# Masked attention and a rational feed-forward layer on one core: other score products, other transfers of queries and keys, and another order

## The chip, the cores and the metric

The kernel runs on one core of a Trainium2 chip. The metric is the device time of one execution in microseconds (us); lower is better. The core has five engines that work side by side: TensorE (PE; its weight loads are PEld), VectorE (DVE), ScalarE (ACT), GpSimd (POOL) and SyncE (SP), which here only issues transfers. DMA engines move the data.

## The reference

There are two stages. The first is attention with a threshold, the second a feed-forward layer whose activation is a quotient of polynomials:

```python
batch, n_heads, seq, head_dim = (8, 8, 576, 64)
scores = scale * np.matmul(q, k.transpose(0, 1, 3, 2))
thresh = np.max(scores, axis=-1, keepdims=True) - tau
scores = np.where(scores >= thresh, scores, -1000000000.0)
attn = np.exp(scores - np.max(scores, axis=-1, keepdims=True))
attn = attn / (np.sum(attn, axis=-1, keepdims=True) + 1e-09)
x = np.matmul(attn, v)            # then laid out as (8 * 576, 512)

n_tokens, d_model, d_ff = (4608, 512, 2048)
h = x @ w_in
P = a[0] + a[1] * h + a[2] * h**2 + a[3] * h**3
Q = 1.0 + np.abs(b[0]) * np.abs(h) + np.abs(b[1]) * h**2
out = (P / (Q + 1e-6)) @ w_out
```

All inputs and the output are 32-bit floats.

## The kernel before

**Units and visits.** Heads go in pairs: 8 batches of 4 pairs, 32 pairs in all (index `bp`). The 576 query rows of a pair are four blocks of 128 and a rest of 64. A *unit* is one block of one pair. A full unit (`t < NT`, `NT` = 4) has 128 rows for both heads; the unit of the rest (`t == NT`) has the 64 rows of both heads on 128 partitions. There are 128 full units and 32 of the rest. Each batch is gone through in two rounds: a *visit* loads the queries and keys of a pair and does two of its blocks, or the two others and the rest (seven visits a batch, as the last pair does all in one). There are 56 visits.

**A unit.** `f_qk` computes the scores into three banks of PSUM, `f_max` their maximum (VectorE, line 815), `f_thr` the threshold, `f_pre` (ScalarE, line 830) and `f_sum` (line 834) the masked exponentials and their sums, `f_rec` the reciprocal, `f_hi` and `f_lo` (lines 339 and 856) the probabilities as two 16-bit halves, `f_tp` (line 866) turns each half by a transposing transfer on SyncE into the tile `pT`, and `f_av` (line 925) multiplies by V. Units of the first batch (`plain`) turn the probabilities on TensorE instead (lines 879 and 884). The score products of a full unit are two 32-bit products of 64 contraction rows, one per head, with 512 keys each (line 805), and one of all 128 rows for the last 64 keys of both heads (line 809). For that one the key tile has blocks of zeros, so that each head's rows meet only its own keys.

**Feed-forward.** `moe_ops` takes 256 tokens and 512 hidden columns at a time: 16-bit products (line 1042), the rational function on ScalarE and VectorE (lines 1051 to 1092), and 32-bit products (line 1101). It runs between the attention units, and for the last tokens alone at the end.

**Loads.** Two tiles QQ hold queries and two tiles KK hold keys (`NQ` = 2). `load_ops` issues three transfers for the queries of a visit and three for its keys, and two more of 16 KB where the visit has a unit of the rest. They are issued by SyncE for the first eight pairs (`EARLY_BP`), the keys of pairs 0 and 1 by ScalarE (`FROM_ACT`), and all others by GpSimd, whose queue also has the loads of V and of the weights and most stores.

**Order.** A planner (`Plan.order`) writes out the order of all instructions on each engine before the kernel is built. Each operation has an engine or a choice of two (`FLEX`), an assumed duration, a key and the buffers that it takes and gives back. The planner starts what can start first, and among near equals what has the lower key. `TURN` has an offset of the key for each group of operations, `KIND` one for each kind; `EARLY` and `PRICE` weigh ScalarE against VectorE where an operation may go to either. A transfer on SyncE (`"DMA"`) or GpSimd (`"GD"`) is taken to have landed 2.3 or 2.7 us after its assumed duration, however many others are under way; before 120 us (`LOADS_END`) transfers on SyncE that give a buffer back count double and one more.

Of the kernel before, what the change touches and what calls it, by code (L numbers as in the profile page):

```python
# [16 lines left out]
AX = mybir.AxisListType  # L17

# [19 lines left out]
SINGLE = 21  # L38
# [12 lines left out]

FROM_ACT = 2
# [25 lines left out]
EARLY = {"ACT": 1.2900, "DVE": 3.3863}  # L78
EARLY_END = 714.5248
PRICE = {"ACT": 1.0645, "DVE": 2.1978}  # L80

TURN = [
# [21 lines left out]
KIND = [  # L104
# [8 lines left out]
LOADS_END = 120.0  # L113
# [22 lines left out]
class Plan:  # L136
# [20 lines left out]
    def op(self, eng, dur, key, fn, after=(), take=(), drop=()):  # L157
        engs = {eng: dur} if isinstance(eng, str) else eng
        o = Op(engs, key, fn, [x for x in after if x is not None], list(take), list(drop))
        o.turn, o.kind = self.turn, self.kinds.setdefault(fn.__code__, len(self.kinds))  # L160
        turn = TURN[o.turn] / 1000 if o.turn < len(TURN) else 0.0
        o.key += turn
        o.key += KIND[o.kind] / 1000 if o.kind < len(KIND) else 0.0
        o.rank = self.rank + turn
        self.ops.append(o)
        return o
# [20 lines left out]
    def order(self):  # L187
# [19 lines left out]
        left = len(self.ops)  # L207
        while left:
# [38 lines left out]
            if e == "DMA" and o.drop and t < LOADS_END:  # L247

                o.dur = 2.0 * o.dur + 1.0
            free[e] = end = t + o.dur  # L250
            busy[e] += o.dur
            seen = end + self.LAT[e]
            for h in o.take:
                if h.sets is None:
                    slots = self.pools[h.pool]
                    h.slot = min(slots)[1]
                    slots.remove(min(slots))
                else:
                    h.bank = self.spot(h, t)[1]
                    for i in h.bank:  # L260
                        self.banks[i] = None
                if h.pool in line:
                    line[h.pool].pop()
# [8 lines left out]
            for d in o.then:  # L272
                d.wait -= 1
                for x in d.engs:
                    d.ready[x] = max(d.ready[x], end + (self.OWN[e] if x == e else self.TO.get((e, x), self.LAT[e])))
                    if not d.wait:
                        can[x].append(d)
# [12 lines left out]
def masked_attention_rational_ffn(  # L290
# [86 lines left out]
    QW = S + REM  # L377
    QQs = [const.tile([P, QW], F32, name=f"QQ{i}") for i in range(NQ)]
    KKs = [const.tile([P, QW + REM], F32, name=f"KK{i}") for i in range(NQ)]
    for t in QQs:  # L380
        nc.gpsimd.memset(t[:, NT * P:], 0.0)
    for t in KKs:
        nc.gpsimd.memset(t[0:D, S:QW], 0.0)
        nc.gpsimd.memset(t[D:P, 0:REM], 0.0)
# [96 lines left out]
    def decode_ops(i, key, load, hold, dst=None):  # L481
# [6 lines left out]
        def ld():  # L488
            if not loaded:

                for x in KKs[0][:, REM:REM + 1], QQs[0][:, 0:1]:
                    nc.gpsimd.tensor_scalar(cf[:, 15:16], x, 1.0, 1.0, ALU.mult, ALU.mult)
            if len(loaded) >= AHEAD and plan.now - loaded[-AHEAD][1] < RECENT:


                nc.gpsimd.tensor_scalar(cf[0:1, 15:16], loaded[-AHEAD][0][0:1, 0, 1:2].bitcast(F32), 1.0, 1.0, ALU.mult, ALU.mult)
            box["rw"] = load()
            loaded.append((box["rw"], plan.now))
# [26 lines left out]
        l = op("GD", 2.5, key - 2.0, ld, (), [hold])  # L525
# [112 lines left out]
    def load_ops(bp, ts):  # L638
# [7 lines left out]
        queue, eng = (nc.sync, "DMA") if bp < EARLY_BP else (nc.gpsimd, "GD")  # L646

        def ldq():
# [3 lines left out]
            queue.dma_start(QQ[D:P, S:], qT[bb, pr, :, S:S + REM])  # L652

        def ldk():
            KK = KKs[kh.slot]
            kq_ = nc.scalar if bp < FROM_ACT else queue
            kq_.dma_start(KK[0:D, REM:S], kT[bb, pr, :, 0:NT * P])
            kq_.dma_start(KK[D:P, REM:QW], kT[bb, pr, :, S + REM:])
            kq_.dma_start(KK[0:D, 0:REM], kT[bb, pr, :, NT * P:S])
            if NT in ts:  # L660
                for i in range(2):
                    kq_.dma_start(KK[i * D:(i + 1) * D, QW:], kT[bb, pr, :, NT * P + i * REM:S + i * REM])

        q_done[bp] = [op(eng, 4.3 if first else 1.6, p0, ldq, (), [qh])]
        k_done[bp] = [op(eng, 0.1 if bp < FROM_ACT else 1.6, p0 + 0.1, ldk, (), [kh])]

# [13 lines left out]
    def load_v_ops(bp):  # L680
# [25 lines left out]
        l = v_loaded[bp] = op(eng, 1.6, max(q, V0 + V1 * pr), ld, (), [vhold])  # L706
# [56 lines left out]
    def unit_ops(bp, t):  # L763
# [3 lines left out]
        single = units.index((bp, t)) < SINGLE  # L767
# [18 lines left out]
        def f_qk():  # L786
# [5 lines left out]
            if not full:  # L792

                s = box["s"][0] = s[:, 0:S]
                for k0, c0, n in (REM, 0, NT * P), (QW, NT * P, REM):
                    nc.tensor.matmul(s[:, c0:c0 + n], QQ[:, NT * P:QW], KK[:, k0:k0 + n], **one)
# [4 lines left out]
            for hh in range(2):  # L801

                r = slice(hh * D, (hh + 1) * D)
                d = s[:, 0:NT * P] if hh == 0 else s[:, w - NT * P:]
                nc.tensor.matmul(d, QQ[r, t * P:(t + 1) * P], KK[r, REM:S], **one)  # L805

            dst, src = (bass.AP(x.tensor, x.offset, [list(x.ap[0]), [n, 2], [1, REM]])
                        for x, n in ((s[:, NT * P:S], w - 2 * NT * P - REM), (KK[:, 0:REM], S)))
            nc.tensor.matmul(dst, QQ[:, t * P:(t + 1) * P], src, **one)  # L809
# [138 lines left out]
        qk = op("PE", 1.47 if full else 1.12, p, f_qk, need, [sh[0]], [kh, qh] * nh)  # L948
# [25 lines left out]
        else:  # L974
# [4 lines left out]
            if not full:  # L979
# [3 lines left out]
                    [hi_hold])  # L983
            tp = op("DMA", TPD if full else 0.6 * TPD, p + 0.65, lambda: f_tp("lo"), los + [tp], (), [e_hold])
# [25 lines left out]
    def moe_ops(ck, f0, nb, p, begins, ends, soon):  # L1010
# [161 lines left out]
        if ends:  # L1172
# [4 lines left out]
            for tt in range(2):  # L1177
# [9 lines left out]
                if through:  # L1187
                    op("DMA" if late else "GD", 0.6 if kind == "m" else 1.1, p + 2.3, lambda tt=tt: f_st(tt), [o], (), [ho])
# [95 lines left out]
```

## Time and profile before

| | |
|---|---|
| Median of 3 runs | 1310.31 us (1304.87 to 1311.28) |
| The profiled execution: time, span | 1312.41 us, 1310.6 us |
| Granted clock of TensorE, mean | 0.986 |
| Busy: TensorE, VectorE, ScalarE, GpSimd | 1253.8, 1217.9, 1114.4, 243.4 us |
| Mean busy share of transfers: queue of SyncE and ScalarE, queue of GpSimd | 37.4%, 16.4% of 16 engines |
| Moved | 146.66 MB, of which 60.30 read from HBM and 9.44 written |

The profile is of one execution; a busy time is the time in which at least one instruction of the engine ran. Ends of matmuls are modelled. A row of a timeline begins with the start (us from the first instruction), then the time, the engine, the line and the operation, and "x4" means four merged instructions. An engine name with a q (SPq) is its queue, where it issues transfers. A 32-bit product of line 805 or 809 stands as two records, one for each of its two passes.

### The profile page before, as it was taken

The numbers are of one execution on the slowest core, as the hardware profiler recorded it, in microseconds if no ns is written. First come the engines' busy times: TensorE is split into PE (matmuls) and PEld (weight loads), VectorE is DVE, ScalarE is ACT, GpSimd is POOL, SyncE is SP. The second block draws the span as 40 slices with busy tenths as digits, with TensorE's granted clock in tenths as the row PEclk, the third lists the DMA queues.
The fourth block names the chain that finished last, engine by engine and source line by source line (L and its number), as shares of the span: only waits on it lengthen the run. The fifth ranks groups of instructions, "written<-read, shape, count | busy, mean of one in ns | idle before, by whom it ended". The sixth has DMA issues, their size and how long they took to land. (4 is left out here: it accounts for less than half of the span.)

```text
span 1310.6 us, 25351 instructions
## 1 busy us (share of the span) xinstructions
PE 1253.8 (96%) x9430; PEld 931.8 (71%) x9430; DVE 1217.9 (93%) x1913; ACT 1114.4 (85%) x2182; POOL 243.4 (19%) x462
## 2 busy tenths in 40 slices
PE   8898989999999999998999979999999999999998
PEld 6576677777677777776777657766677777778886
DVE  5899999999999999988999979999999999999777
ACT  5898998999999999997999878978998798885564
POOL 1101100023213220323112231223213221110000
PEclk8998999999999999999999989999999999999999
DMA  7433454476656565677554875676756654563000
GB/s 206 132 116 125 142 128 87 105 160 119 124 116 134 124 131 107 117 143 129 95 103 96 115 132 100 122 126 119 137 106 115 132 131 75 109 111 55 17 17 17
DMA packets 340587, 146.66 MB, mean 112 GB/s; under 512 B 316208, under 2 KB 323184, under 8 KB 340464
## 3 DMA queue, kind: packets, MB, share of 16 engines
q1 hardware_dynamic: 316400, 86.49, 37.4%
q0 software_dynamic: 22784, 57.31, 16.4%
q8 instruction: 74, 1.21, 0.4%
q10 hardware_dynamic: 1280, 1.25, 0.4%
q14 instruction: 49, 0.40, 0.1%
HBM read 60.30 MB, written 9.44 MB: 53 GB/s over the span
## 5 line engine op out<-in xcount | busy, mean ns | idle before, releaser
L1101 PE MATMUL banks<-wp,g 128*128 128x512 f32 x1728 | 442.1, 404 | 1.6 <-DVE g L1092 1.2
L1042 PEld LDWEIGHTS <-wi 128*128 128x128 f16 x3456 | 333.6, 98 | 67.1 <-issue 29.0
L1042 PE MATMUL banks<-x,wi 128*128 128x256 f16 x3072 | 360.8, 274 | 10.0 <-ACT t L1051 9.3
L1101 PEld LDWEIGHTS banks<-wp,g 128*128 128x128 f32 x1728 | 315.9, 189 | 75.3 <-DVE g L1092 4.0
L834 ACT ACTIVATE e<-e,cf 128x576 f32<-128x576 f32 x288 | 222.1, 778 | 0.2
L856 DVE SCALAR_TENSOR_TENSOR e<-e,st,hi 128x576 f16<-128x576 f32 x252 | 204.6, 812 | 7.5 <-ACT hi L339 6.4
L339 ACT ACTIVATE hi<-e,st 128x576 f16<-128x576 f32 x223 | 169.6, 769 | 46.8 <-DVE st L845 30.8
L830 ACT ACTIVATE e<-banks,st 128x576 f32<-128x576 f32 x288 | 206.3, 737 | 3.0 <-DMA pT<-e 0.8
L815 DVE TENSOR_REDUCE st<-banks 128x2 f32<-128x1152 f32 x128 | 172.4, 1347 | 16.2 <-PE banks L809 15.8
L805 PE MATMUL banks<-KK,QQ 64*128 64x512 f32 x512 | 154.0, 650 | 7.2 <-DVE t L346 3.9
L925 PE MATMUL banks<-pT,V 128*64 128x256 f16 (+1 forms) x2520 | 122.8, 250 | 12.8 <-DMA pT<-e 10.2
L1051 ACT ACTIVATE t<-banks,hsc 128x512 f32<-128x512 f32 (+1 forms) x192 | 106.1, 574 | 30.3 <-PE banks L1042 24.5
L925 PEld LDWEIGHTS <-V 128*64 128x64 f16 x2520 | 105.0, 111 | 34.0 <-issue 22.7
L809 PEld LDWEIGHTS banks<-KK,QQ 128*128 128x128 f32 x256 | 38.6, 190 | 99.1 <-issue 94.6
L1078 DVE SCALAR_TENSOR_TENSOR t<-t,co,t 128x1024 f32<-128x1024 f32 (+1 forms) x73 | 92.3, 1265 | 17.4 <-ACT t L1072 17.1
L1069 ACT ACTIVATE t<-t,co 128x1024 f32<-128x1024 f32 (+1 forms) x73 | 82.8, 1134 | 29.6 <-DVE t L1065 24.1
L1092 DVE TENSOR_TENSOR g<-t,g 128x512 fp32r<-128x512 f32 x144 | 95.0, 684 | 3.1 <-ACT g L331 2.9
L650 POOL DMA_DIRECT2D QQ<-in_qT_dram x42 | 22.2, 529 | 381.0 <-PE banks L809 194.8
L1084 DVE SCALAR_TENSOR_TENSOR t<-t,co,t 128x1024 f32<-128x1024 f32 (+1 forms) x73 | 92.3, 1265 | 0.6
L1075 DVE SCALAR_TENSOR_TENSOR t<-t,co,t 128x1024 f32<-128x1024 f32 (+1 forms) x73 | 92.2, 1264 | 0.1
L1065 DVE SCALAR_TENSOR_TENSOR t<-t,co 128x1024 f32<-128x1024 f32 (+1 forms) x73 | 92.3, 1264 | 0.0
L1062 DVE SCALAR_TENSOR_TENSOR t<-t,co 128x1024 f32<-128x1024 f32 (+1 forms) x73 | 92.2, 1263 | 0.0
(128 smaller groups left out, 1545.3 us busy)
## 6 DMA issues: line engine op xcount, KB each, us to landing
t<-in_w_in_dram POOLq DMA_DIRECT2D x16, 512.0 KB, 5.3
t<-in_w_out_dram POOLq DMA_DIRECT2D x16, 512.0 KB, 4.1
out_dram<-u POOLq DMA_DIRECT2D x26, 256.0 KB, 2.9
V<-in_v_dram POOLq DMA_DIRECT2D x24, 256.0 KB, 4.5
QQ<-in_qT_dram POOLq DMA_DIRECT2D x42, 144.0 KB, 2.8
KK<-in_kT_dram POOLq DMA_DIRECT2D x42, 144.0 KB, 3.2
QQ<-in_qT_dram POOLq DMA_DIRECT2D x42, 128.0 KB, 2.9
KK<-in_kT_dram POOLq DMA_DIRECT2D x42, 128.0 KB, 2.8
```

The lines of the kernel that those rows point to most:

```text
L339: nc.scalar.activation(dst, src, AF.Identity, scale=factor)
L805: nc.tensor.matmul(d, QQ[r, t * P:(t + 1) * P], KK[r, REM:S], **one)
L815: nc.vector.tensor_reduce(box["st"][:, 0:2], box["both"], AX.X, ALU.max, negate=True)
L830: nc.scalar.activation(ev(hh), box["s"][hh], AF.Prelu, scale=SCALE, bias=box["st"][:, 2 + hh:3 + hh], alpha=STEEP)
L834: nc.scalar.activation(e, e, AF.Exp, scale=passes, accum_out=box["st"][:, 4 + hh:5 + hh])
L856: nc.vector.scalar_tensor_tensor(box["lo"][:, c], ev(hh), box["st"][:, 6 + hh:7 + hh], box["hi"][:, c], ALU.mult, ALU.subtract)
L925: nc.tensor.matmul(dst, V[:, c * P + hh * D:c * P + (hh + 1) * D], rhs, start=c == 0 and n == 0, stop=c == NT and n == 2)
L1042: nc.tensor.matmul(d, wi_tile(c, f0 + j, hl), x[:, c, :], start=c == 0 and n == 0, stop=c == NC - 1 and n == 2)
L1051: nc.scalar.activation(box["h3"][:, 2 * k:2 * k + 2, sl], psv[:, :, sl], AF.Identity, scale=hsc[:, b2, g:g + 1])
L1065: nc.vector.scalar_tensor_tensor(box["q"], box["q"], bc, box["q"], ALU.add, ALU.mult)
L1092: nc.vector.tensor_tensor(fr(g[:, 1]), box["r"][:, k * GW:(k + 1) * GW], g[:, 0], ALU.subtract)
L1101: nc.tensor.matmul(acc[tt], fr(g[:, x]), fr(wo[f][y]), start=begins and j == n == 0, stop=ends and j == nb - 1 and n == 2)
```

## The change

Full units' scores become four products of 64 contraction rows: 64 keys of the first head, 512 of the second, 512 of the first, 64 of the second. The two products of 64 keys write one PSUM bank, so an empty instruction on TensorE before the fourth waits for the first. The key tile loses its blocks of zeros and its second copy of the last 64 keys. Each head's keys come in one transfer; the third transfer of the queries is issued only where the visit has a unit of the rest. All queries and keys are issued by SyncE (`EARLY_QK` = 32), but for the keys of the first visits of pairs 0 and 1, which stay with ScalarE; V, weights and stores stay where they were. In the planner, transfers carry a `wire` pair: the first number is time on a wire that all of them share, the second the time from then to landing. All numbers of `TURN`, `KIND`, `EARLY` and `PRICE` are new, except `EARLY_END`. The change's name also speaks of sums of exponentials in SBUF.

```diff
+EARLY_QK = 32
-EARLY = {"ACT": 1.2900, "DVE": 3.3863}
+EARLY = {"ACT": 1.4369, "DVE": 3.4200}
-PRICE = {"ACT": 1.0645, "DVE": 2.1978}
+PRICE = {"ACT": 1.0733, "DVE": 2.2524}
...
-LOADS_END = 120.0
+BEGIN = 1.4
...
-            if e == "DMA" and o.drop and t < LOADS_END:
-
-                o.dur = 2.0 * o.dur + 1.0
             free[e] = end = t + o.dur
             busy[e] += o.dur
             seen = end + self.LAT[e]
+            if o.wire is not None:
+                wire = max(wire, t + BEGIN) + o.wire[0]
+                seen = max(wire, end + 1.0) + o.wire[1]
...
-                    d.ready[x] = max(d.ready[x], end + (self.OWN[e] if x == e else self.TO.get((e, x), self.LAT[e])))
+                    d.ready[x] = max(d.ready[x], seen if o.wire is not None else
+                                     end + (self.OWN[e] if x == e else self.TO.get((e, x), self.LAT[e])))
...
-    QW = S + REM
-    QQs = [const.tile([P, QW], F32, name=f"QQ{i}") for i in range(NQ)]
-    KKs = [const.tile([P, QW + REM], F32, name=f"KK{i}") for i in range(NQ)]
+    QQs = [const.tile([P, S + REM], F32, name=f"QQ{i}") for i in range(NQ)]
     for t in QQs:
         nc.gpsimd.memset(t[:, NT * P:], 0.0)
-    for t in KKs:
-        nc.gpsimd.memset(t[0:D, S:QW], 0.0)
-        nc.gpsimd.memset(t[D:P, 0:REM], 0.0)
+    KKs = [const.tile([P, S], F32, name=f"KK{i}") for i in range(NQ)]
...
-        queue, eng = (nc.sync, "DMA") if bp < EARLY_BP else (nc.gpsimd, "GD")
+        act = bp < FROM_ACT and ts[0] == 0
+        queue, eng = (nc.sync, "DMA") if bp < EARLY_QK else (nc.gpsimd, "GD")
...
-            queue.dma_start(QQ[D:P, S:], qT[bb, pr, :, S:S + REM])
+            if NT in ts:
+                queue.dma_start(QQ[D:P, S:], qT[bb, pr, :, S:S + REM])
 
         def ldk():
-            KK = KKs[kh.slot]
-            kq_ = nc.scalar if bp < FROM_ACT else queue
-            kq_.dma_start(KK[0:D, REM:S], kT[bb, pr, :, 0:NT * P])
-            kq_.dma_start(KK[D:P, REM:QW], kT[bb, pr, :, S + REM:])
-            kq_.dma_start(KK[0:D, 0:REM], kT[bb, pr, :, NT * P:S])
-            if NT in ts:
-                for i in range(2):
-                    kq_.dma_start(KK[i * D:(i + 1) * D, QW:], kT[bb, pr, :, NT * P + i * REM:S + i * REM])
+            kq_ = nc.scalar if act else queue
+            for hh, c in (0, 0), (1, S + REM):
+                kq_.dma_start(KKs[kh.slot][hh * D:(hh + 1) * D, :], kT[bb, pr, :, c:c + S])
...
-            for hh in range(2):
-
+            for hh, k0, n, d0 in (0, NT * P, REM, NT * P), (1, 0, NT * P, w - NT * P), (0, 0, NT * P, 0), (1, NT * P, REM, w - S):
                 r = slice(hh * D, (hh + 1) * D)
-                d = s[:, 0:NT * P] if hh == 0 else s[:, w - NT * P:]
-                nc.tensor.matmul(d, QQ[r, t * P:(t + 1) * P], KK[r, REM:S], **one)
-
-            dst, src = (bass.AP(x.tensor, x.offset, [list(x.ap[0]), [n, 2], [1, REM]])
-                        for x, n in ((s[:, NT * P:S], w - 2 * NT * P - REM), (KK[:, 0:REM], S)))
-            nc.tensor.matmul(dst, QQ[:, t * P:(t + 1) * P], src, **one)
+                if d0 == w - S:
+
+                    tc.add_manual_dep(nc.tensor.nop().ins, shared.ins.name, ORDERED, reason="one bank")
+                mm = nc.tensor.matmul(s[:, d0:d0 + n], QQ[r, t * P:(t + 1) * P], KK[r, k0:k0 + n], **one)
+                if d0 == NT * P:
+                    shared = mm
...
-        qk = op("PE", 1.47 if full else 1.12, p, f_qk, need, [sh[0]], [kh, qh] * nh)
+        qk = op("PE", 1.36 if full else 1.12, p, f_qk, need, [sh[0]], [kh, qh] * nh)
```

The tables `TURN` and `KIND` are left out here. The `wire` pairs are (0.75, 1.0) for queries, keys and stores, (0.95, 1.5 or 2.5) for V, (1.75, 2.0) for a weight block and (1.2, 0.8) for a transpose of a full unit, (0.65, 0.8) for one of the rest.

More of the change, by code (lines that the diff above doesn't have):

```diff
@@ L17 @@
 AX = mybir.AxisListType
+ORDERED = mybir.DependencyInfo(mybir.DependencyClass.Sync, mybir.DependencyReason.DATA)
 REBIAS = 2.0 ** -112
@@ L155, in pool, with op @@
         self.pools[name] = [(0.0, i) for i in range(n)]
-    def op(self, eng, dur, key, fn, after=(), take=(), drop=()):
+    def op(self, eng, dur, key, fn, after=(), take=(), drop=(), wire=None):
         engs = {eng: dur} if isinstance(eng, str) else eng
         o = Op(engs, key, fn, [x for x in after if x is not None], list(take), list(drop))
+        o.wire = wire
         o.turn, o.kind = self.turn, self.kinds.setdefault(fn.__code__, len(self.kinds))
@@ L206, in order @@
         done, busy = [], dict.fromkeys(engines, 0.0)
-        left = len(self.ops)
+        left, wire = len(self.ops), 0.0
         while left:
@@ L489, in ld @@
             if not loaded:
-                for x in KKs[0][:, REM:REM + 1], QQs[0][:, 0:1]:
+                for x in KKs[0][:, 0:1], QQs[0][:, 0:1]:
                     nc.gpsimd.tensor_scalar(cf[:, 15:16], x, 1.0, 1.0, ALU.mult, ALU.mult)
@@ L523, in f6 @@
                 tensor_tensor(dst.bitcast(I32), t, box["rw"][:, :, 0], ALU.add)
-        l = op("GD", 2.5, key - 2.0, ld, (), [hold])
+        l = op("GD", 2.5, key - 2.0, ld, (), [hold], wire=(1.75, 2.0))
         if i < NC:
@@ L651, in ldq @@
             queue.dma_start(QQ[D:P, 0:NT * P], qT[bb, pr, :, S + REM:])
-            queue.dma_start(QQ[D:P, S:], qT[bb, pr, :, S:S + REM])
+            if NT in ts:
+                queue.dma_start(QQ[D:P, S:], qT[bb, pr, :, S:S + REM])
         def ldk():
-            KK = KKs[kh.slot]
-            kq_ = nc.scalar if bp < FROM_ACT else queue
-            kq_.dma_start(KK[0:D, REM:S], kT[bb, pr, :, 0:NT * P])
-            kq_.dma_start(KK[D:P, REM:QW], kT[bb, pr, :, S + REM:])
-            kq_.dma_start(KK[0:D, 0:REM], kT[bb, pr, :, NT * P:S])
-            if NT in ts:
-                for i in range(2):
-                    kq_.dma_start(KK[i * D:(i + 1) * D, QW:], kT[bb, pr, :, NT * P + i * REM:S + i * REM])
-        q_done[bp] = [op(eng, 4.3 if first else 1.6, p0, ldq, (), [qh])]
-        k_done[bp] = [op(eng, 0.1 if bp < FROM_ACT else 1.6, p0 + 0.1, ldk, (), [kh])]
+            kq_ = nc.scalar if act else queue
+            for hh, c in (0, 0), (1, S + REM):
+                kq_.dma_start(KKs[kh.slot][hh * D:(hh + 1) * D, :], kT[bb, pr, :, c:c + S])
+        issue = {"DMA": 1.25, "GD": 1.1}[eng]
+        q_done[bp] = [op(eng, 3.1 if first else issue + (0.6 if NT in ts else 0.0), p0, ldq, (), [qh], wire=(0.75, 1.0))]
+        k_done[bp] = [op(eng, 0.1 if act else issue, p0 + 0.1, ldk, (), [kh], wire=(0.75, 1.0))]
+    place_of = {u: i for i, u in enumerate(units)}
     def is_plain(bp, t):
@@ L705, in load_v_ops @@
         q = bp * (NT + 0.5) - 17.0
-        l = v_loaded[bp] = op(eng, 1.6, max(q, V0 + V1 * pr), ld, (), [vhold])
+        l = v_loaded[bp] = op(eng, 1.7, max(q, V0 + V1 * pr), ld, (), [vhold], wire=(0.95, 1.5 if eng == "DMA" else 2.5))
         hv = [Hold("u", 1)]
@@ L766, in unit_ops @@
         full = t < NT
-        single = units.index((bp, t)) < SINGLE
+        single = place_of[bp, t] < SINGLE
         heads = (0, 1) if full else (0,)
@@ L794, in f_qk @@
                 s = box["s"][0] = s[:, 0:S]
-                for k0, c0, n in (REM, 0, NT * P), (QW, NT * P, REM):
-                    nc.tensor.matmul(s[:, c0:c0 + n], QQ[:, NT * P:QW], KK[:, k0:k0 + n], **one)
+                for c0, n in (0, NT * P), (NT * P, REM):
+                    nc.tensor.matmul(s[:, c0:c0 + n], QQ[:, NT * P:], KK[:, c0:c0 + n], **one)
                 return
@@ L982, in unit_ops @@
             tp = op("DMA", TPD if full else 0.6 * TPD, p + 0.6, lambda: f_tp("hi"), his + two["tp"], [two["pT"]] if t % 2 == 0 else (),
-                    [hi_hold])
-            tp = op("DMA", TPD if full else 0.6 * TPD, p + 0.65, lambda: f_tp("lo"), los + [tp], (), [e_hold])
+                    [hi_hold], wire=(1.2 if full else 0.65, 0.8))
+            tp = op("DMA", TPD if full else 0.6 * TPD, p + 0.65, lambda: f_tp("lo"), los + [tp], (), [e_hold], wire=(1.2 if full else 0.65, 0.8))
             two["tp"].append(tp)
@@ L1187, in moe_ops @@
                 if through:
-                    op("DMA" if late else "GD", 0.6 if kind == "m" else 1.1, p + 2.3, lambda tt=tt: f_st(tt), [o], (), [ho])
+                    op("DMA" if late else "GD", 0.6 if kind == "m" else 1.1, p + 2.3, lambda tt=tt: f_st(tt), [o], (), [ho], wire=(0.75, 1.0))
                 else:
```

49 rows, old and new, of tables (KIND, TURN) are left out of this document.

## The prediction

> **What bounds the kernel now.** I read the page's head first, then busy time by stretch, then the waits of each engine, then the instructions around one score product and one late transpose.
>
> ```profile
> span 1310.6 us, 25351 instructions
> PE 1253.8 (96%) x9430; PEld 931.8 (71%) x9430; DVE 1217.9 (93%) x1913; ACT 1114.4 (85%) x2182; POOL 243.4 (19%) x462
> ```
>
> Columns of the next view, by stretch: length, then busy time (and count) of PE, PEld, DVE, ACT, POOL, then TensorE's granted clock, the DMA engines' share and GB/s.
>
> ```profile
> 0.00:100.00 100.00, 87.08 (x583) 63.72 (x584) 80.69 (x198) 81.05 (x180) 14.14 (x43) 0.95 0.51 150
> 100.00:700.00 600.00, 580.74 (x4427) 427.21 (x4426) 576.93 (x905) 547.54 (x1088) 118.44 (x217) 0.99 0.59 122
> 700.00:800.00 100.00, 90.03 (x700) 65.75 (x699) 87.83 (x134) 79.27 (x165) 27.66 (x50) 0.95 0.63 111
> 800.00:1170.00 370.00, 360.47 (x2779) 264.73 (x2779) 358.19 (x545) 323.40 (x617) 82.05 (x150) 1.00 0.61 117
> 1170.00:1310.00 140.00, 135.49 (x960) 110.39 (x954) 114.25 (x135) 83.17 (x137) 1.12 (x2) 1.00 0.14 29
> ```
>
> TensorE and VectorE are both nearly full from 100 to 1170 us (97% and 96% in the first long stretch), so a saving on one alone is worth about half until the other stops it. The end (from 1170 us) is feed-forward alone, with TensorE at 97%; nothing of the change acts there but the order. What could be won by order alone is what both lose: TensorE is idle for 57 us of the span, VectorE for 93. The waits say how much of it hangs on transfers (columns: who waited, for whom: us in total, times, longest):
>
> ```profile
> PE banks L925 <- DMA pT<-e: 10.2, 9, 5.2
> PE banks L1042 <- ACT t L1051: 9.8, 8, 2.6
> DVE x L941 <- ACT x L935: 9.9, 3, 6.1
> ACT u L703 <- DMA V<-in_v_dram: 10.1, 9, 3.8
> ACT hi L339 <- DMA pT<-hi: 9.1, 3, 3.5
> ACT pT L331 <- issue: 2.3, 1, 2.3
> POOL QQ L650 <- PE banks L809: 194.8, 20, 25.7
> ```
>
> Of line 866, the transposes, the view of one line says who waited for them and how long one takes to land:
>
> ```profile
>   PE banks L925: 11.6, 10
>   ACT hi L339: 9.1, 3
> DMA to landing us min/median/max: 2.5/3.4/11.3
> ```
>
> Ten of 280 transposes come too late for TensorE, 11.6 us in all, and ScalarE loses 9.1 us to three. The largest, 5.2 us, has its cause beside it:
>
> ```profile
> 748.67 0.53 POOL L657 DMA_DIRECT2D KK<-in_kT_dram  x1
> 754.42 0.53 POOL L650 DMA_DIRECT2D QQ<-in_qT_dram  x1 [4.18 <-PE banks L809]
> 753.26 2.37 SPq L866 DMA_TRANSPOSE pT<-e  x1
> ```
>
> Two visits' queries and keys go out within 10 us, and the transpose between them takes 2.37 us to issue instead of its usual 1.3. The old plan, for which a transfer lands 2.3 us after it ends on its queue whatever else is moving, can't see that.
>
> **The change part by part.** *The score products.* Durations: one group on TensorE, its inner starts, and what follows it.
>
> ```profile
> 602.84 0.70 PE L805 MATMUL banks<-KK,QQ 64*128 64x512 f32 x2
> 603.37 0.60 PE L805 MATMUL banks<-KK,QQ 64*128 64x512 f32 x2
> 603.90 0.38 PE L809 MATMUL banks<-KK,QQ 128*128 128x128 f32 x1
> 604.11 0.28 PE L809 MATMUL banks<-KK,QQ 128*128 128x128 f32 x1
> 604.14 0.48 PE L1101 MATMUL banks<-wp,g 128*128 128x512 f32 x1
> 861.82 1.13 PE L805 MATMUL banks<-KK,QQ 64*128 64x512 f32 x4
> 863.21 1.47 PE L1042 MATMUL banks<-x,wi 128*128 128x256 f16 x12
> 410.45 1.13 PE L805 MATMUL banks<-KK,QQ 64*128 64x512 f32 x4
> 411.92 0.63 PE L925 MATMUL banks<-pT,V 128*64 128x256 f16 x8
> ```
>
> A product is two passes. The two heads' 64-row products run side by side: both first passes start at 602.84, both second ones at 603.37. A first pass of 512 columns takes 0.53 us, one of 128 columns 0.21 (603.90 to 604.11), so a column costs 0.32/384 = 0.83 ns and the rest, the weight load, 0.107. A second pass has its load under the first: 0.107 + 2 x 0.427 = 0.96 for the 512 columns, then 0.10 until 603.90, the change from half rows to full rows, then another bare load and 2 x 0.107. From the group's start to the next group's it is 1.30 us (before line 1101), 1.39 (line 1042), 1.47 (line 925).
>
> New, per half: one product of 64 columns and one of 512. Load 0.107, passes of 0.053; the next loads (0.107) are only half hidden under these, 0.054 bare each; then 2 x 0.427: 0.107 + 0.053 + 0.054 + 0.053 + 0.054 + 0.854 = 1.175, and 0.10 for the change back to full rows, which now comes after the group instead of inside it: 1.27. Against 1.30, 1.39 and 1.47 that is 0.03, 0.12 or 0.20 saved, and as the next group's first weight load then lies bare, where it was partly hidden, less than that before lines 1042 and 1101. I take 0.06 of bounds 0 and 0.20: with 128 groups (256 records of line 809), 8 us of TensorE time, half of which reaches the end: **-4**. On the bad side, if nothing overlaps as above, a half takes 2 x 0.160 + 2 x 0.533 = 1.39, plus 0.10: 1.49, which is 0.02 to 0.19 lost.
>
> The wait (an empty instruction before the fourth product, until the first is done, as both write one bank) holds all of TensorE's queue behind it. The first is over after 0.27 us, the second and third run to 0.96 and 1.17, so 0.7 us of work covers it; without that cover it would cost what the signal takes, 128 times. I put it at 0. VectorE's maximum waits for the same end of the group as before.
>
> The Trainium skill speaks against this part: TensorE: Matmul & The Clock Gate, "Part 3: Packing small matmuls", says that matmuls start and end strictly in program order. By it the third product could not start before the second's second pass. In the rows above the second head's first pass starts with the first head's first, ahead of that one's second pass, which bears more on products than on passes; so it stays a rival below.
>
> *The loads.* Rows of the groups and of two queues:
>
> ```profile
> L650 POOL DMA_DIRECT2D QQ<-in_qT_dram x42 | 22.2, 529 | 381.0 <-PE banks L809 194.8 <-PE banks L796 181.8 <-PE banks L1101 4.4
> L662 POOL DMA_DIRECT2D KK<-in_kT_dram x48 | 26.0, 552 | 0.2 <-issue 0.2
> 72.44 0.60 SPq L651 DMA_DIRECT2D QQ<-in_qT_dram  x1
> L866 SPq DMA_TRANSPOSE pT<-hi x140: 1200/1292/2063, 177.3 to 1189.2; - x140
> 45.81 2.16 ACTq L662 DMA_DIRECT2D KK<-in_kT_dram  x2
> ```
>
> After the first eight head pairs there are 42 visits with six issues each and 48 more small ones: 300 issues on GpSimd. They become 42 x 4 + 24 = 192 on SyncE at 0.60 us, 115 us. SyncE has 280 transposes at 1.3 (364 us) and some early loads, so it is under half full; what counts is what stands behind what. A load of a visit holds SyncE for 4.6 x 0.60 = 2.7 us, and longer if its buffer isn't free yet; behind it stand transposes, and behind these TensorE's line 925. On GpSimd such a load stands for long (194.8 us on line 809 alone), with V's loads, the weights and the stores behind it: those go free, and ScalarE waits 10.1 us for V. The bytes stay as they were but for the second copy of the last 64 keys. ScalarE issues 12 transfers less; five of them (43.86 to 48 us) kept it from a ready copy for 2.3 us. For the first load, one 16 KB transfer less of queries and of keys saves about 0.6 us before the first product. I take **-2** for ScalarE, **-1** for V and the start. Move to SyncE by itself: between -5 (all of V's wait that lies before a busy ScalarE) and +23 (rival below); I take 0, as the planner now orders these loads between the transposes with its own times for them. Removed memsets on GpSimd lie at the start under the first loads: 0.
>
> The skill's DMA: Bandwidth & Descriptors, "Issuing engines are not separate DMA queues", says that transfers of all issuing engines share the same 16 DMA engines, and only issue time is saved. The trace agrees: 2.8 us to landing for queries from GpSimd, 3.2 from SyncE:
>
> ```profile
> QQ<-in_qT_dram POOLq DMA_DIRECT2D x42, 144.0 KB, 2.8
> QQ<-in_qT_dram SPq DMA_DIRECT2D x14, 144.0 KB, 3.2
> ```
>
> *The plan.* Its transfers now queue for one wire, and all offsets and prices are new. No row shows the new order; bounds are what the old one loses: 11.6 + 9.1 = 21 us to late transposes on the good side, and as much again on the bad side, since the new table fits a model too. Nearest is the wait of TensorE itself, which is on a full engine; I take most of it, **-9**. *Sums of exponentials in SBUF*: lines 834 and 839 already sum into the tile st, which lies in SBUF, and the diff leaves them; so 0.
>
> Sum: -4 - 2 - 1 - 9 = -16. The profiled execution took 1312.4 us (span 1310.6 and 1.8 around it), 0.2% above the median of 1310.3: **1296**.
>
> **The rivals.** (a) *The order wins more*: all 21 us of late transposes go, 0.10 us or more of each group (13), 2 of ScalarE: -36 at full worth, -30 with VectorE in the way: 1281. For: both engines idle together at 760 us. Against: VectorE at 96% has no work taken off it. (b) *No change*: VectorE binds, the score saving vanishes and late transposes only move: 1307, give or take 4. For: the 9.8 us behind line 1051 and most other waits have nothing to do with transfers. (c) *SyncE as the bound, slower*: loads stand ahead of transposes, 42 x 2.7 = 115 us of delay handed to pT; if a fifth of it reaches TensorE, +23, less 7 for the rest: 1328. It decides from the point where more than one visit in ten finds pT with less than 2.7 us to spare; today ten transposes of 280 have none. (d) *Products in program order, slower*: 1.49 us a group, 0.10 to 0.19 more for the usual followers, 128 x 0.14 = 18 us on TensorE, of which three quarters reach the end (13), less 5 for the order: 1320. This is also the time that the page's rule would give.
>
> **How the numbers follow.** Forecast 0.42 (its own range 1287 to 1303), (a) 0.18, (b) 0.20, (c) 0.12, (d) 0.08. Half a per cent, about what a measurement here tells from no change, is 1303.8 to 1316.9. Faster 0.42 + 0.18 = 0.60, same 0.20, slower 0.20. Leaving out half of (a) and the worse half of (c) and (d), the range is 1274 to 1322.
>
> **What would show it.** The score group: four products with all starts of the third about 0.3 us after the group's, and 1.27 us to the next group; 1.49 says (d). On SyncE: direct transfers between transposes; TensorE's wait for pT under 5 us says the plan term is right, over 20 says (c). GpSimd's wait on QQ gone, ScalarE's 2.3 us gone. TensorE's busy time near 1246 and VectorE's unchanged. The forecast is wrong if TensorE's and VectorE's idle times in 100 to 1170 us stay as they are, or if a new wait for KK or QQ appears before the scores.

## The result, and the profile after

The changed kernel took 1291.05 us (median of 4 runs, 1289.5 to 1296.84) against 1309.2 us for the kernel before on the same chip (median of 4 runs): a ratio of 0.9886, 95% interval 0.9855 to 0.9917. That is 18 us faster, and 5 us under the forecast of 1296. The profiled execution took 1291.3 us, with a span of 1289.5.

The head of the page, and busy time by stretch in the same stretches and columns as before:

```profile
span 1289.5 us, 25792 instructions
PE 1233.6 (96%) x9668; PEld 966.1 (75%) x9668; DVE 1218.6 (95%) x1935; ACT 1110.6 (86%) x2159; POOL 83.8 (6%) x159
```

```profile
0.00:100.00 100.00, 83.75 (x567) 66.28 (x568) 81.33 (x201) 82.20 (x182) 14.80 (x41) 0.91 0.52 153
100.00:700.00 600.00, 581.09 (x4633) 451.60 (x4633) 585.39 (x929) 549.17 (x1082) 38.15 (x66) 1.00 0.59 121
700.00:800.00 100.00, 94.25 (x796) 73.59 (x795) 94.21 (x152) 86.02 (x168) 9.58 (x16) 1.00 0.52 109
800.00:1170.00 370.00, 360.34 (x2918) 280.73 (x2916) 362.87 (x557) 331.50 (x631) 21.23 (x36) 0.99 0.61 119
1170.00:1289.00 119.00, 114.19 (x762) 93.86 (x760) 94.84 (x100) 61.68 (x100) 0.00 (x0) 1.00 0.08 21
```

VectorE does the same work in less time: 1218.6 us busy against 1217.9, so its idle time fell by 22 us, most of it between 100 and 800 us. TensorE lost 20 us of busy time and kept its idle time, 56 us against 57. Looked at from TensorE alone, the whole gain would be shorter products; this reading is one of the theories below, and it is wrong.

The waits and the transposes (the last three rows are from the view of line 865, the transposes):

```profile
PE banks L1041 <- ACT t L1050: 8.2, 9, 1.4
PE banks L1100 <- ACT u L1111: 7.1, 2, 5.5
PE banks L806 <- DMA KK<-in_kT_dram: 3.6, 3, 1.6
PE banks L806 <- DMA QQ<-in_qT_dram: 2.9, 2, 2.1
ACT u L703 <- DMA V<-in_v_dram: 0.8, 1, 0.8
SPq L651 <- PE banks L796: 87.6, 22, 28.1
SPq L651 <- PE banks L806: 63.7, 20, 19.5
  ACT hi L343: 4.7, 3
  PE banks L924: 2.1, 3
DMA to landing us min/median/max: 2.5/3.3/6.7
```

TensorE's wait for late transposes fell from 11.6 to 2.1 us, ScalarE's from 9.1 to 4.7, and the latest transpose lands after 6.7 us instead of 11.3. ScalarE's wait for V fell from 10.1 to 0.8. The loads now stand on SyncE for 151 us until their buffer is free, with transposes behind them, and nothing shows that this hurts. One sign that the prediction named against itself did appear: TensorE's products wait 6.5 us for keys and queries in front of the scores, against 0.8 before (its weight loads waited 5.3 us then and 1.8 now). 5.8 of the 6.5 us lie in the first 28 us. One group of score products (rows of a timeline that overlap one moment each, so "x3" are those then running):

```profile
697.30 0.70 PE L806 MATMUL banks<-KK,QQ 64*128 64x64 f32 x2
697.57 1.07 PE L806 MATMUL banks<-KK,QQ 64*128 64x512 f32 x3
697.84 0.81 PE L806 MATMUL banks<-KK,QQ 64*128 64x512 f32 x4
698.58 0.50 PE L1100 MATMUL banks<-wp,g 128*128 128x512 f32 x1
```

The group starts at 697.30, the third product 0.27 us later, the second product's second pass at 697.84, and the next group at 698.58: 1.28 us, in front of each kind of follower. The working had 1.27.

### The profile page after: what moved, and what is told of

Its sections match the earlier page's. It is cut to its first block, busy times and chain, and to the rows that moved or that the text cites. A ratio compares the mean times of both kernels' runs of the same rounds, so it can differ in the third digit from the quotient of the medians.

```text
span 1289.5 us, 25792 instructions
## 1 busy us (share of the span) xinstructions
PE 1233.6 (96%) x9668; PEld 966.1 (75%) x9668; DVE 1218.6 (95%) x1935; ACT 1110.6 (86%) x2159; POOL 83.8 (6%) x159
## 4 chain that ended last, share of the span: by engine, by line
PE 26%; DVE 22%; issue 5%; ACT 4%; DMA 2%; SPq 0%; DVEq 0%; ACTq 0%
PE banks L1100 11%; PE banks L1041 8%; DVE e L855 4%; PE banks L806 3%; PE banks L924 3%; DVE t L1077 2%; DVE t L1080 2%; DVE st L814 2%; DVE t L1064 2%; DVE g L1091 2%; DVE t L1083 2%; DVE t L1061 2%; DVE t L1074 2%; DMA pT<-hi 1%; PE banks L796 1%
## 5 line engine op out<-in xcount | busy, mean ns | idle before, releaser
L1041 PEld LDWEIGHTS <-wi 128*128 128x128 f16 x3456 | 328.9, 98 | 72.0 <-issue 30.1
L806 PE MATMUL banks<-KK,QQ 64*128 64x64 f32 (+1 forms) x1024 | 175.7, 454 | 10.9 <-ACT e L829 4.4
L806 PEld LDWEIGHTS banks<-KK,QQ 64*128 64x128 f32 x1024 | 115.8, 187 | 81.4 <-issue 47.8
L1080 DVE SCALAR_TENSOR_TENSOR t<-t,t 128x1024 f32<-128x1024 f32 (+1 forms) x73 | 87.8, 1203 | 0.6
```

Source lines behind the costliest of these rows:

```text
L806: mm = nc.tensor.matmul(s[:, d0:d0 + n], QQ[r, t * P:(t + 1) * P], KK[r, k0:k0 + n], **one)
L1041: nc.tensor.matmul(d, wi_tile(c, f0 + j, hl), x[:, c, :], start=c == 0 and n == 0, stop=c == NC - 1 and n == 2)
```

## The experiments

Three theories stood at the start. **P**, the prediction's sum: products 4 us, ScalarE's issues, V and the start 3, the move to SyncE nothing by itself, order 9. **G**: the products are the whole gain, as TensorE's busy time says. **O**: the order is the whole gain. In the runs of the changed kernel "order kept" means that the planner saw the same operations, times and engines, and so wrote the same order, while the instructions issued differ. Of each edit only the main lines are printed.

**Old products in the new order.** `f_qk`, the padded key tile, the key transfers and the third query transfer of before, in the changed kernel:

```diff
-            for hh, k0, n, d0 in (0, NT * P, REM, NT * P), (1, 0, NT * P, w - NT * P), (0, 0, NT * P, 0), (1, NT * P, REM, w - S):
+            for hh in range(2):
...
+            nc.tensor.matmul(dst, QQ[:, t * P:(t + 1) * P], src, **one)
```

> The changed kernel with the old three score products per full unit, their padded key tile and their key transfers; the order of all operations stays that of the changed kernel. Theory P (the prediction's sum: products 4 us, order 9): TensorE's group goes from 1.28 back to 1.30 to 1.48, 5 to 8 us more of TensorE's busy time, and 1291 becomes 1295 to 1298. Theory G (TensorE's busy time fell by 20 us and its idle time did not, so the products are the whole gain): 1305 to 1311. Theory O (the order is the whole gain): 1291, give or take 2.

Measured: 1312.13 us, 1.0041 (1.0021 to 1.0062) of the kernel before. It is 20 us slower than the changed kernel, as G said, and even slower than before. But it also issues 709 transfers and transposes on SyncE instead of 567, and TensorE's wait for transposes is back at 11.0 us:

```profile
PE banks L934 <- DMA pT<-e: 11.0, 7, 4.0
```

**Loads back on GpSimd, order kept.**

```diff
-        queue, eng = (nc.sync, "DMA") if bp < EARLY_QK else (nc.gpsimd, "GD")
+        queue, eng = (nc.sync if bp < EARLY_BP else nc.gpsimd), "DMA"
```

> The changed kernel, order kept, with the queries and keys from the ninth pair on issued by GpSimd instead of SyncE. Theory P: the queue by itself is worth nothing, 1289 to 1294. Rival Q (on GpSimd these loads hold up V, weights and stores, which SyncE relieved): 1297 or more, with ScalarE's wait for V back at 10 us. Rival H (on SyncE they hold up the transposes, so the changed kernel pays for the move): 1285 or less, with the transposes' waits of 7 us gone.

Measured: 1302.41 us, 0.9960 (0.9939 to 0.9982). Rival Q: the move is worth something by itself, 0.74% here. The waits give part of it:

```profile
PE banks L924 <- DMA pT<-e: 5.0, 6, 1.8
ACT u L703 <- DMA V<-in_v_dram: 3.2, 4, 1.6
PE 1235.3 (95%) x9668; PEld 966.3 (75%) x9668; DVE 1220.3 (94%) x1935; ACT 1110.7 (86%) x2159; POOL 186.0 (14%) x351
```

TensorE waits 2.9 us more for transposes and ScalarE 2.4 us more for V than in the changed kernel; the 10 us that Q named for V did not come back. VectorE's busy time is 1.7 us longer.

**The new order alone:** both edits together, so that the old products and loads run in the new order.

> The new order alone: old products, old key transfers and loads on GpSimd, in the changed kernel's order. Theory P: 9 to 12 us below the kernel before, 1297 to 1300, and the waits for the transposes well under the 21 us of before. Theory G: 1309, as before. Theory O: 1291.

Measured: 1303.21 us, 0.9979 (0.9956 to 1.0002). The order alone is worth about 3 us, with an interval that just reaches nothing, and O and P are both off; G, which gave it nothing, comes nearest. This run and the first differ in the queue of the late loads alone: with the old transfers, SyncE is slower than GpSimd by 8 us (1.0041 against 0.9979).

```profile
  ACT hi L343: 8.5, 4
  PE banks L934: 1.4, 3
```

The wait of TensorE for transposes did fall, from 11.6 to 1.4 us, nearly as far as in the changed kernel. It bought only those 3 us.

**The new products alone:** four products, one key transfer per head, the third query transfer only where needed; the order and queues of before.

> The kernel before with the four new products, one key transfer per head and the third query transfer only where needed; order and queues as before. Theory P: 4 to 8 us below the kernel before, 1301 to 1305. Theory G: 18 us below, 1291. Theory O: 1309, no change. TensorE's group should be 1.28 us in all cases.

Measured: 1301.78 us, 0.9961 (0.9937 to 0.9985): 5 us, as P said and not G. TensorE's busy time fell by 15.6 us all the same:

```profile
PE 1238.2 (95%) x9686; PEld 969.0 (75%) x9686; DVE 1217.4 (94%) x1913; ACT 1115.4 (86%) x2182; POOL 186.0 (14%) x350
```

So two thirds of what busy time shows as saved is not in the end. G falls: start to start the group shrinks by 0.03, 0.11 or 0.20 us, after it the next group's first weight load lies bare, and VectorE is as full as TensorE.

**More transfers.** The changed kernel with each head's keys in two transfers and the third query transfer always:

```diff
-            if NT in ts:
-                queue.dma_start(QQ[D:P, S:], qT[bb, pr, :, S:S + REM])
+            queue.dma_start(QQ[D:P, S:], qT[bb, pr, :, S:S + REM])
...
+                cuts = [(0, S)] if act else [(0, NT * P), (NT * P, S)]
+                for x, y in cuts:
+                    kq_.dma_start(KKs[kh.slot][hh * D:(hh + 1) * D, x:y], kT[bb, pr, :, c + x:c + y])
```

> The changed kernel with its own products and order, but each head's keys in two transfers (512 and 64 columns) and the third query transfer for every visit: the same bytes of keys, about 130 issues more on SyncE (some 700 in all, as many as the run with the old products had there). Theory T (what the run with the old products lost, 20 us against the changed kernel, is SyncE's time in front of the transposes, not the products): 0.998 to 1.004 of the kernel before, with TensorE waiting 8 us or more for the transposes. Theory G (the products were it): 0.987 to 0.991, as the changed kernel.

Measured: 1301.82 us, 0.9971 (0.9954 to 0.9988), between the two theories' bands; its interval reaches T's, and T's sign, 8 us or more of waits for transposes, is there. It is 0.85% or 11 us above the changed kernel for 132 issues more, 0.08 us of the end each. Of the 20 us of the first run this is a little over half; some 9 are left to the products, on a SyncE nearly as full (699 issues against 709). TensorE waits for transposes again:

```profile
PE banks L925 <- DMA pT<-e: 9.9, 10, 3.1
PE banks L807 <- DMA QQ<-in_qT_dram: 5.2, 2, 4.5
```

**Loads on GpSimd, planned there.**

```diff
-EARLY_QK = 32
+EARLY_QK = 8
```

> The changed kernel with queries and keys from the ninth pair on given to GpSimd in the plan too, so that the order is made for it; products, tables and key transfers as changed. Theory S (the move to SyncE is itself worth about 0.7%): 0.994 to 0.997 of the kernel before, as with the order kept. Rival K (in the run with the order kept the loads only stood at the wrong places of GpSimd's queue): 0.987 to 0.991.

Measured: 1330.41 us, 1.0198 (1.0168 to 1.0228): outside both bands. The tables of offsets were made for another plan, and most of the 40 us that it loses against the changed kernel may come from that, since the run with the old tables below loses as much with the loads on SyncE. TensorE is idle for 83 us of a span of 1333.9, and its longest waits are for ScalarE, not for transfers.

```profile
PE banks L806 <- ACT e L829: 16.9, 14, 4.6
PE banks L1041 <- ACT t L1050: 14.2, 15, 4.1
```

This run doesn't tell S from K; the run with the old order below does.

**The wait without its cover.** The two products of 512 keys first, the two of 64 last:

```diff
-            for hh, k0, n, d0 in (0, NT * P, REM, NT * P), (1, 0, NT * P, w - NT * P), (0, 0, NT * P, 0), (1, NT * P, REM, w - S):
+            for hh, k0, n, d0 in (0, 0, NT * P, 0), (1, 0, NT * P, w - NT * P), (0, NT * P, REM, NT * P), (1, NT * P, REM, w - S):
```

> The changed kernel with the two products of 512 keys first and the two of 64 last, so that the wait on the shared bank has no cover: the fourth product must wait for the end of the third. By the prediction's working the group takes 0.107 + 0.854 + 0.16 + the signal + 0.27 + 0.10, 1.49 and the signal (0.1 to 0.3 us) instead of 1.28: 128 x 0.3 to 0.5 us more on TensorE, half to all of it at the end, ratio 1.005 to 1.03 of the kernel before. Rival (the wait costs nothing even uncovered, or TensorE has room): 0.987 to 0.993.

Measured: 1326.93 us, 1.0163 (1.0139 to 1.0186), 36 us over the changed kernel. The group:

```profile
712.23 0.70 PE L806 MATMUL banks<-KK,QQ 64*128 64x512 f32 x2
712.76 0.76 PE L806 MATMUL banks<-KK,QQ 64*128 64x512 f32 x4
713.25 0.27 PE L806 MATMUL banks<-KK,QQ 64*128 64x64 f32 x1
713.58 0.32 PE L806 MATMUL banks<-KK,QQ 64*128 64x64 f32 x1
713.94 0.50 PE L1100 MATMUL banks<-wp,g 128*128 128x512 f32 x1
```

1.71 us from group to group. The third product's second pass starts at 713.25 and, at 0.053 us, is over at 713.30; the fourth product starts only at 713.58. The signal from TensorE to itself takes 0.28 us. So the wait was worth covering, and in the changed kernel it is covered.

**The old order on the new instructions:** the run of the new products alone, with all late loads issued by SyncE at the places that the old plan had chosen for GpSimd.

```diff
-        queue, eng = (nc.sync, "DMA") if bp < EARLY_BP else (nc.gpsimd, "GD")
+        queue, eng = (nc.sync, "DMA") if bp < EARLY_BP else (nc.sync, "GD")
```

> The kernel before, order kept, with the new products and key transfers and with all late queries and keys issued by SyncE, at the places that the old plan chose for GpSimd: everything of the change on the chip but the new order and the second visits of pairs 0 and 1. Theory R (the order is worth about 10 us, as forecast, but only together with the move: a load that is not planned on SyncE stands ahead of transposes): 0.995 to 1.005 of the kernel before, with waits for the transposes of 15 us or more. Theory N (the order is worth 3 us or less, as the run with old products on GpSimd suggests): 0.987 to 0.991.

Measured: 1293.77 us, 0.9909 (0.9885 to 0.9934), near theory N. The waits that R named are all there, as long as before the change:

```profile
  PE banks L917: 12.1, 10
  ACT hi L340: 10.8, 5
PE 1233.8 (95%) x9686; PEld 965.3 (75%) x9686; DVE 1216.7 (94%) x1913; ACT 1114.8 (86%) x2182; POOL 85.0 (7%) x158
```

23 us of waits for transposes against 7 in the changed kernel, and the end differs by 3 us.

**The wire with the old tables:** `TURN`, `KIND`, `EARLY` and `PRICE` of before in the changed kernel.

```diff
-EARLY = {"ACT": 1.4369, "DVE": 3.4200}
+EARLY = {"ACT": 1.2900, "DVE": 3.3863}
...
-PRICE = {"ACT": 1.0733, "DVE": 2.2524}
+PRICE = {"ACT": 1.0645, "DVE": 2.1978}
...
```

> The changed kernel, its planner with the wire, with the old numbers of TURN, KIND, EARLY and PRICE. If the wire in the plan is what makes the order good: 0.99 to 0.997 of the kernel before. If the tables are fitted to one plan and a plan without its own tables is bad whatever its model, as the run with the loads planned on GpSimd suggests (1.02): 1.01 to 1.03.

Measured: 1335.32 us, 1.0228 (1.0203 to 1.0253). A better model of the transfers doesn't make a good order with numbers that were fitted to another model. What the wire by itself is worth can't be had from this run.

**One transfer each.** Host layout with both heads on 128 partitions; queries with zeros in the block of the rest; order kept:

```diff
-            queue.dma_start(QQ[0:D, 0:S], qT[bb, pr, :, 0:S])
-            queue.dma_start(QQ[D:P, 0:NT * P], qT[bb, pr, :, S + REM:])
-            if NT in ts:
-                queue.dma_start(QQ[D:P, S:], qT[bb, pr, :, S:S + REM])
+            n = S + REM if NT in ts else NT * P
+            queue.dma_start(QQ[:, 0:n], qT[bb, pr, :, 0:n])
...
-            for hh, c in (0, 0), (1, S + REM):
-                kq_.dma_start(KKs[kh.slot][hh * D:(hh + 1) * D, :], kT[bb, pr, :, c:c + S])
+            kq_.dma_start(KKs[kh.slot], kT[bb, pr])
```

> The changed kernel with queries and keys laid out so that one transfer of 128 partitions brings both heads' keys and one both heads' queries (with the zeros of the rest's block where the visit has a rest): two issues a visit instead of four or five, some 140 fewer on SyncE; order kept. Theory T (issues on SyncE ahead of the transposes cost 0.1 us of the end each): 0.980 to 0.985 of the kernel before. Rival (at the changed kernel's count the transposes are early enough already, their waits are 7 us in all): 0.986 to 0.991.

Measured: 1287.0 us, 0.9857 (0.9831 to 0.9882), between the two bands, with an interval that reaches both. So it ran again beside the changed kernel on one chip, four executions and five:

> The changed kernel itself, on the same chip as the run with one transfer each: 0.986 to 0.992 of the kernel before.

> One transfer of 128 partitions for both heads' keys and one for their queries, order kept, beside the changed kernel. If the issues on SyncE that it saves (142) still cost 0.03 us each of the end: 0.983 to 0.988, 3 to 5 us under the changed kernel. If the first run was a matter of the chip: the same as the changed kernel within 2 us.

Measured: the changed kernel 1290.39 us, 0.9886 (0.9863 to 0.9908); one transfer each 1285.39 us, 0.9844 (0.9822 to 0.9866). No run of the one (1284.71 to 1286.79) is as long as any of the other (1289.78 to 1292.74). It beats both kernels, by 5 us the changed one.

```profile
KK<-in_kT_dram SPq DMA_DIRECT2D x54, 288.0 KB, 3.4
QQ<-in_qT_dram SPq DMA_DIRECT2D x32, 320.0 KB, 3.1
QQ<-in_qT_dram SPq DMA_DIRECT2D x24, 256.0 KB, 3.1
```

Twice the bytes land 0.3 to 0.4 us later than half of them did. The Trainium skill has this as a rule, DMA: Bandwidth & Descriptors, "Rules for kernel authors": two transfers to disjoint partition halves run on the same engines, so one of 128 partitions is to be used. The trace agrees, with 142 issues less and 5 us.

**Together**, in shares of the kernel before (each has an interval of about 0.2% either way, so a difference of two has 0.3%, 4 us; the steps of 2.5 and 3 us are not told from nothing):

| step | from the old order | from the new order |
|---|---|---|
| products and fewer transfers | 1 to 0.9961: 5 us | 0.9979 to 0.9960: 2.5 us |
| loads to SyncE | 0.9961 to 0.9909: 7 us | 0.9960 to 0.9886: 10 us |
| order, with the second visits of pairs 0 and 1 | 0.9909 to 0.9886: 3 us | 1 to 0.9979: 3 us |

**The granted clock lies in these shares too.** In the 52 executions of the kernel before that ran beside the experiments, a lower mean clock goes with a longer time: twelve at 0.984 to 0.987 took 1309.2 us on average, eleven at 0.992 to 0.994 took 1303.6, about 1 us for each 0.001. The steps are not compared at one clock. The new products alone had 0.985 to 0.990 (mean 0.988), the same with the loads on SyncE 0.992 to 0.994 (0.993); the changed kernel with its loads on GpSimd 0.983 to 0.989 (0.987), the changed kernel 0.986 to 0.991 (0.990); the new order alone 0.990, the kernel before 0.990. Two rows of the old order, from 700 to 1000 us, the loads on GpSimd and then on SyncE (the clock is the third number from the end):

```profile
700.00:1000.00 300.00, 288.46 (x2308) 223.56 (x2306) 289.59 (x444) 264.30 (x512) 58.33 (x105) 0.98 0.61 117
700.00:1000.00 300.00, 288.68 (x2350) 223.94 (x2351) 292.03 (x449) 267.36 (x523) 21.82 (x37) 1.00 0.62 119
```

As an estimate from these numbers, at one clock the move would be worth 2 us from the old order and 7 from the new, and the order 6 us and 3. In the profile before, the clock is 0.50 for five stretches of 3.4 or 6.8 us after 100 us, 27 us in all; in the one after there are two, 10 us in all. Each stands behind idle time of TensorE, 1.6 to 3.2 us of the 3.5 ahead of it; the one from 758.3 us begins in the 5.2 us for which TensorE waits for the late transpose that the prediction shows. So a wait may cost TensorE more than the idle time itself. Why the run with 23 us of waits for transposes has the highest clock is not shown, and no run holds the clock fixed.

## Why the prediction was right, and where it was not

**The time** came out by the steps' sum (16 us forecast, 18 measured), but two of its steps were wrong by much and made up for each other, so that the time is in part luck. The range is wider at its lower end than its own words give: with half of rival (a) left out, it would end near that rival's own 1281, not at 1274.

**The score products: right in size, and in price as far as the runs can tell.** 1.27 us a group was worked out, 1.28 measured. -4 for the end stands between 2.5 and 5 (some 9 with SyncE as full as in the first run); these have 3 to 4 us either way, and the fewer transfers are in them. Rival (d), products in program order with 1.49 us, is out: the third product starts 0.27 us after the first, while the second is in its first pass. The rule of the Trainium skill (TensorE: Matmul & The Clock Gate, "Part 3: Packing small matmuls") holds here for the starts of products and not for their passes: the second's second pass starts after the third's first. The forecast that TensorE's busy time would be near 1246 was wrong (1233.6). A busy time with modelled ends is not a sum of starts, and the prediction took it for one; nor is it taken at one clock: with the old products in the new order alone it is 1246.4 us, 7 less than before, with no product changed.

**The wait in TensorE's queue at 0: right.** It has its price when the cover goes: 0.28 us for the signal and more for the loads that can't run ahead, 0.43 us a group in all.

**The move to SyncE at 0: wrong.** This step of the sum failed by 7 to 10 us, to the good side (2 to 7 at one clock, by the estimate above). The prediction gave only a gain of 5 at most, from V's wait. What the traces show of it: TensorE's wait for transposes and ScalarE's for V are 5 us shorter than with the loads on GpSimd, order kept, and VectorE's busy time 1.7 us. As with the order, such waits need not reach the end in full; and in the old order ScalarE's wait for V did not shrink with the move (5.5 and 6.3 us), and TensorE's busy time fell by 4.4 us, its idle time by 0.5. So the cause stays open. Landing times changed little: by the medians, queries take 2.8 to 3.1 us from GpSimd and 2.8 to 2.9 from SyncE, keys 3.2 and 2.9 to 3.0. By the rule of the Trainium skill that the prediction used (DMA: Bandwidth & Descriptors, "Issuing engines are not separate DMA queues": only issue time is saved) it should have been next to nothing; the two pairs of runs differ by 0.5% and 0.7%. Rival (c), loads ahead of transposes, had the right mechanism for another kernel: with 132 issues more on SyncE it costs 11 us. The prediction spread its 115 us of issues over all visits as delay; at the changed kernel's count that delay isn't seen.

**The order at -9: wrong in size.** The wait that it was read from went as forecast (under 5 us was named as its sign, and it is 2.1), but the step from that wait to the end failed. Two orders on nearly the same instructions have 23 and 7 us of waits for transposes and differ by 3 us at the end, or some 6 at one clock. VectorE is 95% full, and where TensorE waits for a transpose VectorE mostly has other work to go on with: it is busy for 11.3 of these 12.1 us with the old order on SyncE, and for 8.5 of the 11.6 before the change.

**ScalarE -2 and V with the start -1:** the 2.3 us behind ScalarE's issues went, and so did 9.3 us of its wait for V; the first score product starts at 7.8 us instead of 8.4, the 0.6 us forecast, but the waits for keys and queries behind it are longer. Neither was tried alone. **Sums of exponentials in SBUF** were there before; nothing to measure.

**What was left out:** the number of issues on SyncE as a price of its own. One key transfer per head stood in the sum as nothing but fewer issues; on SyncE it is what makes the move pay at all: with the old transfers and products, in the new order, the move costs 8 us (3 of them go with the clock, by the same estimate).

## What to carry to other kernels

A wait that ends last on one engine is not a loss of the kernel while another full engine works through it: change the order alone, or the instructions alone, before a sum of waits is booked as a gain. Move transfers to a queue that issues something urgent only with as few issues as can be; here 142 issues less were worth 5 us and 132 more cost 11. A table fitted to one plan is part of that plan: with a changed plan the kernel was 2% slower than before, whichever model was better.

## What the runs showed of the hardware that was not expected

A product of 64 rows starts as soon as its half of the array is free, 0.27 us into a group, while the other half is still in the first of two passes of an earlier product; both halves then run at 0.83 ns a column and pass, and by that price the last, short product is over before the third, long one. TensorE's wait on its own result costs 0.28 us when nothing covers it. Moving 192 load issues from GpSimd to SyncE made the kernel 7 to 10 us faster, part of it with a higher clock, while the loads land at most 0.3 us sooner in the median. The clock granted to TensorE fell to one half for 3.4 or 6.8 us at a time behind 1.6 to 3.2 us of idle time within 3.5, in kernels whose TensorE is 96% busy; between executions of the kernel before, 0.001 of mean clock goes with about 1 us.
